# Feed-forward part in pairs of blocks, biases in pairs, all weights over one load queue, and a new instruction order, in an attention-plus-highway kernel

## The chip, the cores and the metric

The kernel runs on one core of a Trainium2 chip. A core has a matrix engine (TensorE, PE in the profile, with its weight loads as PEld), a vector engine (VectorE, DVE), a scalar engine (ScalarE, ACT), a general engine (GpSimd, POOL), a fifth engine that here only issues transfers (SyncE, SP), and 16 DMA engines that move data between the main memory (HBM), and the on-chip memory (SBUF). Matrix products land in PSUM, eight banks of 512 float32 columns on 128 partitions. The engines run at the same time, each in its own program order, and wait for one another on semaphores. The metric is the device time of one execution, in microseconds (us).

## The reference

```
q, k, v: [8 batches, 8 heads, 576 positions, 64]
scores = q k^T / 8 - slope[h] * |i - j|,   kept only where 0 <= i - j < 128
attn   = softmax(scores) v
x      = attn, heads side by side: [4608 tokens, 512]
H      = relu(x w_h)
T      = sigmoid(x w_t + b_t)
out    = T * H + (1 - T) * x                [4608, 512] float32
```

## The kernel before

**Tiling.** Two batches are done at a time (`m` = 0 to 3). Their 576 positions are five blocks of 128, 128, 128, 128 and 64 positions, and a block of queries meets only its own block of keys and the one before. The work of one `m` is cut into stages: `A` and `B` (key blocks 0-1 and 2-4), or, for `m` = 0, the smaller stages `a`, `b`, `c`, `d`. Within a stage the eight heads are taken two at a time (`g` = 0 to 3).

**Attention.** q and k are loaded by GpSimd's DMA queue, which turns float32 into bfloat16 on the way (`load_qk`, `load_tails` for the last 64 positions, `load_v`). `transposes` (`tr`) brings q and k to head-dimension-first by matrix transposes, `evac` (`te`) copies them out of PSUM on DVE or ACT. `scores` (`s`, L329) multiplies, both batches at once in two halves of 64 array rows each. `soft` (`exp`, L345, ACT) takes the exponential, `mask` (`msk`, L364, DVE) multiplies the band mask in, `pv` (L393) multiplies with v, which carries a column of ones for the sum, and `norm` (`nrm`, L409 and L410, DVE) divides and writes the attention output of one stage, the tile `x`.

**Feed-forward part.** When all heads of a stage are normalised, its blocks of 128 tokens go through, one block (`gi`) at a time:

- `f_x` (`xp`, L433, PE): four transposes of `x`; `f_xe` (`x`, L442, ACT): the copy out of PSUM;
- `f_h` (`h`, L449, PE): four matmuls with `w_h`; `f_u` (`u`, L456, DVE): relu, minus `x`;
- `f_z` (`z`, PE): four matmuls with `w_t` (L465) and a fifth (L467) that adds the bias `b_t` by multiplying a row of ones (`ones1`) with the bias row `bT`; `f_th` (`th`, L473, ACT): tanh;
- `f_t` (`t`, L478, GpSimd): tanh to sigmoid; `f_g` (`g`, L483, DVE): product with `u`; `f_out` (`o`, L489, GpSimd): plus `x`, to float32; `f_st` (`st`, L497 and L505, SP): four stores of 32 partitions each, or two for a last block of 64 positions.

For the second-last blocks of the last stage `t` is on DVE, and the very last `o` too.

**Weights.** `w_t` and `b_t` come over GpSimd's queue. `w_h` is loaded by SP as float32 into the buffer that will later hold the q of `m` = 1 (`wf`, L222), and ACT casts it to bfloat16 (`wc`, L228).

**Order.** Every step above is a node of a list. The program's order, on all engines together, is the written list `ISSUE` of node numbers, and the PSUM bank of each allocation is taken in turn from the written list `BANKS`. Both were made by a search with the planner's costs given in `node(...)`; on the chip only the order and the banks matter. So an engine never overtakes: a node that waits holds up all later nodes of its engine. The functions that the change touches:

Of the kernel before, what the change touches and what calls it, by code (L numbers as in the profile page):

```python
# [14 lines left out]
def kernel(  # L15
# [41 lines left out]
        "A": ((0,), (1,), (2,), (3,)), "B": ((0,), (1,), (2,), (3,), (4,)),  # L57
        "a": ((0,), (1,)), "b": ((0,), (1,)), "c": ((0,), (1,)), "d": ((0,), (1,), (2,)),
    }

# [77 lines left out]
    ones1 = cp.tile([P, P], BF16, name="ones1")  # L138
    wH = cp.tile([P, NCK, DM], BF16, name="wH")
# [51 lines left out]
    def c_vec():  # L191
        nc.vector.memset(ones1[:], 0.0)
        nc.vector.memset(ones1[0:1, :], 1.0)
        nc.vector.memset(bT[:], 0.0)
        for h in range(H):
            nc.vector.memset(cvec[:, h : h + 1], float(np.exp(-float(P) * slopes[h])))
# [20 lines left out]

    def w_stage():
        return QL[1][:].rearrange("p r h n -> p (r h n)").bitcast(F32)

    def load_wf():
        nc.sync.dma_start(  # L222
            out=w_stage().rearrange("p (c n) -> p c n", c=NCK),
            in_=moe_w_h.rearrange("(c p) n -> p c n", p=P),
        )

    def cast_wf():
        nc.scalar.copy(out=wH[:].rearrange("p c n -> p (c n)"), in_=w_stage())  # L228

    def load_w(n):  # L230
        if n == 2:
            nc.gpsimd.dma_start(out=bT[0:1, :], in_=moe_b_t.rearrange("(o n) -> o n", o=1))
        else:
            nc.gpsimd.dma_start(
                out=(wH, wT)[n][:],
                in_=(moe_w_h, moe_w_t)[n].rearrange("(c p) n -> p c n", p=P),
            )
# [177 lines left out]

    def grp(m, kind, gi):
        bs = GROUPS[kind][gi]
# [9 lines left out]
    def f_x(m, kind, gi):  # L427
# [3 lines left out]
        for i in range(n):  # L431
            for c in range(NCK):
                nc.tensor.transpose(  # L433
                    out=pt[:, c * P : (c + 1) * P], in_=x[:, i, c * P : (c + 1) * P],
# [3 lines left out]
    def f_xe(m, kind, gi):  # L438
# [4 lines left out]
            out=xt[:, 0:n].rearrange("p i c n -> p i (c n)"), in_=TR[m, kind, gi][:, 0:512].rearrange("p (i n) -> p i n", i=1)  # L443
        )

    def f_h(m, kind, gi, i):
        AH[m, kind, gi] = ps_tile(1)
        for c in range(NCK):
            nc.tensor.matmul(out=AH[m, kind, gi], lhsT=XT[m, kind, gi][:, i, c, :],  # L449
                             rhs=wH[:, c, :], start=c == 0, stop=c == NCK - 1)  # L450

    def f_u(m, kind, gi):
# [4 lines left out]
            out=uu[:, 0:n, :], in0=AH[m, kind, gi].rearrange("p (i n) -> p i n", i=1), scalar=0.0, in1=x,  # L457
            op0=ALU.max, op1=ALU.subtract,
        )

    def f_z(m, kind, gi, i):
        AZ[m, kind, gi] = ps_tile(1)
        az = AZ[m, kind, gi]
        for c in range(NCK):
            nc.tensor.matmul(out=az, lhsT=XT[m, kind, gi][:, i, c, :], rhs=wT[:, c, :],  # L465
                             start=c == 0, stop=False)
        nc.tensor.matmul(out=az, lhsT=ones1[:], rhs=bT[:], start=False, stop=True)  # L467

    def f_th(m, kind, gi):
# [3 lines left out]
        nc.scalar.activation(out=tt[:, 0:n, :], in_=AZ[m, kind, gi].rearrange("p (i n) -> p i n", i=1), func=ACTF.Tanh,  # L473
# [11 lines left out]
    def f_out(m, kind, gi, eng):  # L485
        bs, n, x = grp(m, kind, gi)
        ot = op.tile([P, 2, DM], F32, name="ot")
        OT[m, kind, gi] = ot
        eng.tensor_tensor(out=ot[:, 0:n, :], in0=UU.pop((m, kind, gi))[:, 0:n, :], in1=x, op=ALU.add)  # L489

    def f_st(m, kind, gi):
        ot, bs = OT.pop((m, kind, gi)), GROUPS[kind][gi]
# [17 lines left out]
    MODES = {"s": (1, 1), "tr": (2, 2), "pvB": (0, 2), "pvd": (0, 2)}  # L510
# [13 lines left out]
    node(("wf",), "SP", 450, -200, load_wf, land=2700)  # L524
    node(("wc",), "ACT", 2200, 2 * T, cast_wf, [("wf",)])
# [17 lines left out]
    def EV(m, w, part):  # L543
# [4 lines left out]
    HALF = {"A": (215, 1118, 1320, 370, 950), "B": (225, 1118, 1320, 800, 1080),  # L548
            "a": (130, 690, 790, 150, 640), "b": (130, 690, 790, 280, 640),
            "c": (130, 690, 790, 280, 640), "d": (160, 690, 790, 520, 800)}  # L550
# [7 lines left out]
    for m in range(ND):  # L558
# [4 lines left out]
        def qk(x=None, hs=None):  # L563
            for w in (0, 1):
# [4 lines left out]
                            lambda m=m, w=w: load_qk(m, w, x, hs), free + [("wc",)] * (m == 1 and w == 0)))  # L569
# [12 lines left out]
        if m == 0:  # L582
# [3 lines left out]
            for n_ in (1, 2):  # L586
                seq.append((("w", n_), 850, 2650 if n_ == 1 else 10, 1, lambda n_=n_: load_w(n_), []))
# [28 lines left out]
        for kind in ORDER[m]:  # L616
# [53 lines left out]
            for gi, bs in enumerate(GROUPS[kind]):  # L670
# [12 lines left out]
                for i in range(n):  # L683
                    node(("h", kb, i), "PE", 800, t + 0.4 * i * dt, lambda kb=kb, i=i: f_h(*kb, i),
                         [("x", kb), ("wc",), ("h", kb, 0)][: 2 + i], take=None if i else 1,
                         uses=[("x", kb)], keep=None if i else "uu")
                node(("u", kb), "DVE", (690, 1220)[two], t + 0.2 * dt, lambda kb=kb: f_u(*kb),
                     [("h", kb, n - 1)], take="uu", uses=[("h", kb, 0), xo])
                for i in range(n):
                    node(("z", kb, i), "PE", 1080, t + (0.5 + 0.4 * i) * dt,  # L690
                         lambda kb=kb, i=i: f_z(*kb, i),
                         [("h", kb, i), ("w", 1), ("w", 2)] + [("z", kb, 0)] * i,
                         take=None if i else 1, uses=[("x", kb)], keep=None if i else "tt")
                node(("th", kb), "ACT", (600, 1120)[two], t + 0.6 * dt, lambda kb=kb: f_th(*kb),
                     [("z", kb, n - 1)], take="tt", uses=[("z", kb, 0)])
                e, cost = ("DVE", (350, 500)) if last and gi else ("POOL", (750, 1350))
# [3 lines left out]
                node(("g", kb), "DVE", (500, 800)[two], t + 0.9 * dt, lambda kb=kb: f_g(*kb),  # L700
                     [("u", kb), ("t", kb)], uses=[("u", kb), ("th", kb)])
                end = last and gi == len(GROUPS[kind]) - 1
                e, cost = ("DVE", (640, 1150)) if end else ("POOL", (1250, 2350))
# [88 lines left out]
```

The softmax here doesn't subtract the row's maximum and nothing guards it: scores larger than these inputs give would overflow.

## Time and profile before

| | |
|---|---|
| median of 3 runs | 175.18 us (175.17 to 175.36) |
| the profiled execution's own time | 175.22 us |
| its span, first to last instruction | 173.5 us |
| PE busy | 150.3 us, 87% |
| DVE, ACT, POOL busy | 140.0, 125.4, 118.1 us |
| moved by GpSimd's queue, by SP's | 14.68 MB, 10.49 MB |
| granted TensorE clock | 0.987 |

Busy time is a sum over instructions. PE's includes the tail of each pipelined matmul, so a PE that is shown busy is not at its peak. The distance from one matmul's start to the next one's is the better measure of what it costs.

### The profile page before, as it was taken

To read this page: it belongs to the slowest core of one execution; us is meant where nothing else is said; L and a number is where in the kernel's file an instruction comes from. 1 tells how busy PE (TensorE), PEld (TensorE's weight loads), DVE (VectorE), ACT (ScalarE), POOL (GpSimd) and SP (SyncE) were. 2 spreads that over 40 slices of the span, in tenths; PEclk is the share of its full clock that TensorE was granted. 3 is DMA by queue.
4 is the path that set the end of the run, shared out by engine and by line. 5 is a ranking of instruction groups with operands and counts; after the bars stand their busy time and mean duration, and the time that the engine had idled before them with its cause. 6 is when DMAs were issued, how large, how long until landed. Compare 5 with 4: busy or idle time off the path is not lost.

```text
span 173.5 us, 5255 instructions
## 1 busy us (share of the span) xinstructions
PE 150.3 (87%) x2132; PEld 92.8 (54%) x2132; DVE 140.0 (81%) x244; ACT 125.4 (72%) x178; POOL 118.1 (68%) x132
## 2 busy tenths in 40 slices
PE   0169789999799789999999979999999999999930
PEld 0158544666566347766556755566556556754410
DVE  5087686999898888999867999889887899976580
ACT  2625678797799969899779968799898897235510
POOL 7997373488883799984067985884485969676540
PEclk9999999999999999999999999999999999999995
DMA  4999999999999999999999996793124332454443
GB/s 161 211 191 191 154 197 185 184 176 102 190 205 202 197 108 158 216 217 210 252 118 154 153 179 97 88 135 99 45 64 121 76 90 68 107 127 113 125 121 91
DMA packets 70167, 25.50 MB, mean 147 GB/s; under 512 B 48128, under 2 KB 65024, under 8 KB 70144
## 3 DMA queue, kind: packets, MB, share of 16 engines
q0 software_dynamic: 62832, 14.68, 120.7%
q1 hardware_dynamic: 7312, 10.49, 22.6%
q8 instruction: 16, 0.26, 0.7%
q14 instruction: 7, 0.06, 0.1%
HBM read 30.41 MB, written 9.44 MB: 230 GB/s over the span
## 4 chain that ended last, share of the span: by engine, by line
PE 53%; DMA 29%; DVE 5%; POOL 4%; ACT 3%; issue 2%; SPq 0%; POOLq 0%; ACTq 0%; DVEq 0%
DMA va<-in_v_dram 17%; PE ps L465 14%; PE ps L449 14%; DMA ktl<-in_k_dram 8%; PE ps L393 7%; PE ps L329 7%; PE ps L271 4%; PE ps L433 4%; DMA kl<-in_k_dram 3%; PE ps L467 3%; ACT pt L345 2%; DVE pt L364 1%; POOL kl L113 1%; DVE uu L456 1%; DMA out_dram<-ot 1%
## 5 line engine op out<-in xcount | busy, mean ns | idle before, releaser
L345 ACT ACTIVATE pt<-ps,bias 128x1024 bf16<-128x1024 f32 (+1 forms) x80 | 72.2, 950 | 13.5 <-PE ps L329 13.2
L489 POOL TENSOR_TENSOR ot<-uu,x 128x512 f32<-128x512 bf16 x35 | 47.7, 1365 | 24.9 <-DVE uu L483 24.8
L364 DVE TENSOR_TENSOR pt<-pt,mk 128x2048 bf16<-128x2048 bf16 (+1 forms) x40 | 46.5, 1174 | 0.8 <-ACT pt L345 0.8
L465 PE MATMUL ps<-wT,xt 128*128 128x512 bf16 x144 | 37.0, 379 | 1.0 <-DVE uu L456 0.8
L449 PE MATMUL ps<-wH,xt 128*128 128x512 bf16 x144 | 37.0, 386 | 0.3 <-DVE qt L290 0.3
L473 ACT ACTIVATE tt<-ps 128x512 f16<-128x512 f32 x36 | 21.6, 602 | 13.0 <-PE ps L467 11.9
L456 DVE SCALAR_TENSOR_TENSOR uu<-ps,x 128x512 bf16<-128x512 f32 x36 | 24.5, 684 | 4.6 <-PE ps L449 4.3
L329 PE MATMUL ps<-qt,kt 64*128 64x256 bf16 (+2 forms) x384 | 24.8, 248 | 3.4 <-DVE qt L290 1.1
L478 POOL TENSOR_SCALAR tt<-tt 128x512 f16<-128x512 f16 x32 | 21.8, 687 | 7.7 <-ACT tt L473 7.5
L410 DVE TENSOR_TENSOR x<-ps,rd 128x256 bf16<-128x256 f32 (+3 forms) x40 | 25.5, 638 | 1.4
L125 POOL DMA_DIRECT2D va<-in_v_dram x20 | 22.3, 1115 | 5.6 <-DMA ql<-in_q_dram 4.2
L393 PE MATMUL ps<-va,pt 128*128 128x65 bf16 (+1 forms) x576 | 24.9, 197 | 0.8 <-DMA va<-in_v_dram 0.7
L393 PEld LDWEIGHTS <-pt 128*128 128x128 bf16 (+1 forms) x576 | 21.1, 101 | 8.2 <-issue 2.9
L442 ACT COPY xt<-ps 128x512 bf16<-128x512 bf16 x36 | 20.7, 589 | 5.3 <-PE ps L433 5.1
L483 DVE TENSOR_TENSOR uu<-uu,tt 128x512 bf16<-128x512 bf16 x36 | 19.1, 538 | 4.3 <-POOL tt L478 4.1
L449 PEld LDWEIGHTS <-xt 128*128 128x128 bf16 x144 | 13.0, 99 | 14.3 <-issue 2.1
L465 PEld LDWEIGHTS <-xt 128*128 128x128 bf16 x144 | 12.9, 98 | 13.6 <-issue 1.5
L329 PEld LDWEIGHTS <-kt 64*128 64x128 bf16 x384 | 13.2, 96 | 12.9 <-issue 8.9
L271 PE MATMUL ps<-ident,kl 128*64 128x128 bf16 (+1 forms) x320 | 12.3, 228 | 8.1 <-DMA kl<-in_k_dram 7.9
L296 ACT COPY kt<-ps 128x1024 bf16<-128x1024 bf16 x13 | 13.0, 1020 | 5.4 <-PE ps L271 5.4
L271 PEld LDWEIGHTS <-kl 128*64 128x64 bf16 (+1 forms) x320 | 9.9, 126 | 10.1 <-DMA kl<-in_k_dram 8.4
L290 DVE COPY qt<-ps 128x1024 bf16<-128x1024 bf16 x16 | 11.0, 686 | 3.8 <-PE ps L271 3.7
(44 smaller groups left out, 125.5 us busy)
## 6 DMA issues: line engine op xcount, KB each, us to landing
out_dram<-ot SPq DMA_DIRECT2D x128, 64.0 KB, 2.4
va<-in_v_dram POOLq DMA_DIRECT2D x16, 256.0 KB, 14.2
ql<-in_q_dram POOLq DMA_DIRECT2D x3, 1024.0 KB, 16.0
kl<-in_k_dram POOLq DMA_DIRECT2D x3, 1024.0 KB, 15.7
ql<-in_moe_w_h_dram SPq DMA_DIRECT2D x1, 1024.0 KB, 5.2
out_dram<-ot SPq DMA_DIRECT2D x8, 128.0 KB, 2.4
kl<-in_k_dram POOLq DMA_DIRECT2D x4, 128.0 KB, 5.5
ql<-in_q_dram POOLq DMA_DIRECT2D x4, 128.0 KB, 5.9
```

Of the source, the lines that this page charges most:

```text
L125: nc.gpsimd.dma_start(out=VA[m % 2][0:n, c, :, :, 0:D].rearrange("s r h d -> s (r h) d"), in_=v[2 * m : 2 * m + 2, :, c * P : c * P + n, : ...
L271: nc.tensor.transpose(out=pt[r * D : (r + 1) * D, c : c + n], in_=L[ps, r, nh * hs + hl, t * D : (t + 1) * D], identity=ident[ps, ps],)
L329: nc.tensor.matmul(out=sc[:, r, o + off : o + off + w_], lhsT=KT[i][rows, h, j * P : (j + 1) * P], rhs=rhs, start=not add, stop=not add or ...
L345: nc.scalar.activation(out=PT[m, home, h // 2][:, h % 2, :, c0 : c0 + W], in_=SC[m, kind, h][:, :, o : o + W], func=ACTF.Exp, bias=BIAS[:, ...
L364: nc.vector.tensor_tensor(out=o, in0=o, in1=mk.to_broadcast([P, 2, rep, W]), op=ALU.mult,)
L393: nc.tensor.matmul(out=av[rows, hl, n * (D + 1) : (n + 1) * (D + 1)], lhsT=pt[:, hl, r, off : off + (D if narrow else P)], rhs=va[:, j, r, ...
L410: nc.vector.tensor_tensor(out=x.rearrange("p b (h d) -> p h b d", h=2), in0=av[:, :, :, 0:D], in1=rd[:, :, 0:nb].to_broadcast([P, 2, nb, D ...
L449: nc.tensor.matmul(out=AH[m, kind, gi], lhsT=XT[m, kind, gi][:, i, c, :], rhs=wH[:, c, :], start=c == 0, stop=c == NCK - 1)
L456: nc.vector.scalar_tensor_tensor(out=uu[:, 0:n, :], in0=AH[m, kind, gi].rearrange("p (i n) -> p i n", i=1), scalar=0.0, in1=x, op0=ALU.max ...
L465: nc.tensor.matmul(out=az, lhsT=XT[m, kind, gi][:, i, c, :], rhs=wT[:, c, :], start=c == 0, stop=False)
L478: eng.tensor_scalar(out=tt, in0=tt, scalar1=0.5, scalar2=0.5, op0=ALU.mult, op1=ALU.add)
L489: eng.tensor_tensor(out=ot[:, 0:n, :], in0=UU.pop((m, kind, gi))[:, 0:n, :], in1=x, op=ALU.add)
```

## The change

The blocks of a stage are taken two at a time through the feed-forward part (`GROUPS`), except in the last stage (`GROUPS_END`), where they stay single. A pair has one `x` copy of 1024 columns, one `u`, one `th`, one `t` and one `g` of double width; its `h` and its `z` each take two PSUM banks. The output sum `o` stays one instruction per block, and the store of a pair is four transfers of double size.

The bias of a pair is no longer a fifth matmul per block. A new step `zb` starts both banks with two matmuls of 64 array rows each, one in each half of the array; the bias row is loaded twice, to partitions 0 and 64 of `bT`, and `hot2` holds ones there. Single blocks keep the fifth matmul.

`w_h` is loaded by GpSimd's queue, cast on the way; the SP load `wf` and ACT's cast `wc` are gone, and with them the wait of the q load of `m` = 1 for the cast.

The last block of the last stage (3,B,4) does its `z`, `th`, `t`, `g`, `o` and store in two column halves of 256.

`ISSUE` and `BANKS` are new: 683 nodes instead of 762, 210 bank allocations instead of 252. The order differs from the first load on: GpSimd's loads begin with the second half of q of `m` = 0, `w_h` and the megabyte of k of `m` = 1 stand ahead of `w_t`, and v's block 1 stands behind `w_t`. The program ends with block (2,B,2), not (3,B,4).

```diff
     GROUPS = {
-        "A": ((0,), (1,), (2,), (3,)), "B": ((0,), (1,), (2,), (3,), (4,)),
-        "a": ((0,), (1,)), "b": ((0,), (1,)), "c": ((0,), (1,)), "d": ((0,), (1,), (2,)),
+        "A": ((0, 1), (2, 3)), "B": ((0, 1), (2, 3), (4,)),
+        "a": ((0, 1),), "b": ((0, 1),), "c": ((0, 1),), "d": ((0, 1), (2,)),
     }
+
+    GROUPS_END = ((0,), (1,), (2,), (3,), (4,))
...
+        nc.vector.memset(hot2[:], 0.0)
+        for i in range(2):
+            nc.vector.memset(hot2[i * D : i * D + 1, :], 1.0)
...
-    def load_wf():
-        nc.sync.dma_start(
...
-    def cast_wf():
-        nc.scalar.copy(out=wH[:].rearrange("p c n -> p (c n)"), in_=w_stage())
-
     def load_w(n):
         if n == 2:
-            nc.gpsimd.dma_start(out=bT[0:1, :], in_=moe_b_t.rearrange("(o n) -> o n", o=1))
+            for i in range(2):
+                nc.gpsimd.dma_start(
+                    out=bT[i * D : i * D + 1, :], in_=moe_b_t.rearrange("(o n) -> o n", o=1)
+                )
...
     def f_h(m, kind, gi, i):
-        AH[m, kind, gi] = ps_tile(1)
+        n = grp(m, kind, gi)[1]
+        if i == 0:
+            AH[m, kind, gi] = ps_tile(n).rearrange("p (i n) -> p i n", i=1) if n == 1 else ps_tile(n)
...
+    def f_zb(m, kind, gi):
+        AZ[m, kind, gi] = ps_tile(2)
+        for i in range(2):
+            rows = slice(i * D, (i + 1) * D)
+            nc.tensor.matmul(out=AZ[m, kind, gi][:, i, :], lhsT=hot2[rows, :], rhs=bT[rows, :],
+                             start=True, stop=False)
+
     def f_z(m, kind, gi, i):
-        AZ[m, kind, gi] = ps_tile(1)
-        az = AZ[m, kind, gi]
+        one = grp(m, kind, gi)[1] == 1
+        if one:
+            AZ[m, kind, gi] = ps_tile(1).rearrange("p (i n) -> p i n", i=1)
+        az = AZ[m, kind, gi][:, i, :]
         for c in range(NCK):
             nc.tensor.matmul(out=az, lhsT=XT[m, kind, gi][:, i, c, :], rhs=wT[:, c, :],
+                             start=one and c == 0, stop=not one and c == NCK - 1)
+        if one:
+            nc.tensor.matmul(out=az, lhsT=ones1[:], rhs=bT[:], start=False, stop=True)
...
+    def e_z(m, kind, gi, hf):
...
+        for c in range(NCK):
+            nc.tensor.matmul(out=az, lhsT=XT[m, kind, gi][:, 0, c, :], rhs=wT[:, c, half(hf)],
                              start=c == 0, stop=False)
-        nc.tensor.matmul(out=az, lhsT=ones1[:], rhs=bT[:], start=False, stop=True)
+        nc.tensor.matmul(out=az, lhsT=ones1[:], rhs=bT[:, half(hf)], start=False, stop=True)
...
-    def f_out(m, kind, gi, eng):
+    def f_out(m, kind, gi, i, eng):
         bs, n, x = grp(m, kind, gi)
-        ot = op.tile([P, 2, DM], F32, name="ot")
-        OT[m, kind, gi] = ot
-        eng.tensor_tensor(out=ot[:, 0:n, :], in0=UU.pop((m, kind, gi))[:, 0:n, :], in1=x, op=ALU.add)
+        if i == 0:
+            OT[m, kind, gi] = op.tile([P, 2, DM], F32, name="ot")
+        eng.tensor_tensor(out=OT[m, kind, gi][:, i, :], in0=UU[m, kind, gi][:, i, :],
+                          in1=x[:, i, :], op=ALU.add)
...
-    node(("wf",), "SP", 450, -200, load_wf, land=2700)
-    node(("wc",), "ACT", 2200, 2 * T, cast_wf, [("wf",)])
...
-                            lambda m=m, w=w: load_qk(m, w, x, hs), free + [("wc",)] * (m == 1 and w == 0)))
+                            lambda m=m, w=w: load_qk(m, w, x, hs), free))
...
-                e, cost = ("DVE", (350, 500)) if last and gi else ("POOL", (750, 1350))
+                e, cost = ("DVE", (350, 600)) if last and gi > 1 else ("POOL", (640, 1070))
...
-                end = last and gi == len(GROUPS[kind]) - 1
-                e, cost = ("DVE", (640, 1150)) if end else ("POOL", (1250, 2350))
+                end = last and gi > 2
+                e, cost = ("DVE", 640) if end else ("POOL", 1160)
```

The two written lists `ISSUE` and `BANKS` are replaced whole.

## The prediction

> **What bounds the kernel now.** I read the page's busy shares first, then its slices, then the chain, then the timeline of PE alone and of all engines in the last 25 us.
>
> ```profile
> PE 150.3 (87%) x2132; PEld 92.8 (54%) x2132; DVE 140.0 (81%) x244; ACT 125.4 (72%) x178; POOL 118.1 (68%) x132
> ...
> PE   0169789999799789999999979999999999999930
> ...
> DMA  4999999999999999999999996793124332454443
> ```
>
> PE is the fullest engine and idle for 23.2 us, of which the table by windows puts 8.2 in the first 10 us, 2.2 in 10 to 20, 0.9 in 20 to 30 and 7.3 after its last matmul at 166.2. Only about 4.5 us of idling lie between 40 and 160. So what counts is when PE starts, what it must do, where it stalls, and what follows its last matmul. The DMA row is full up to about 105 us (24 slices), so the loads are the second bound. The timeline of PE shows the two places where they still stop it after 40 us:
>
> ```profile
> 45.92 0.32 PE L393 MATMUL ps<-va,pt 128*64 128x65 bf16 x7 [0.73 <-DMA va<-in_v_dram]
> ...
> 57.83 0.39 PE L257 MATMUL ps<-ident,ktl 64*128 64x64 bf16 x8 [0.89 <-DMA ktl<-in_k_dram]
> ```
>
> The end, from the timeline of all engines: SP is still issuing the stores of earlier blocks when the last one needs it, and the last `o` is on DVE.
>
> ```profile
> 158.99 10.17 SPq L505 DMA_DIRECT2D out_dram<-ot  x20
> ...
> 168.05 0.69 DVE L489 TENSOR_TENSOR ot<-uu,x 128x512 f32<-128x512 bf16 x1
> 169.25 1.11 SPq L497 DMA_DIRECT2D out_dram<-ot  x2
> ```
>
> [...] Two 64-row scores matmuls of 256 columns run side by side, and the bias matmul of 512 columns takes 0.22 us to the next start when a 128-row operation follows, but 0.31 when the 64-row scores follow:
>
> ```profile
> 31.02 0.38 PE L467 MATMUL ps<-bT,ones 128*128 128x512 bf16 x1
> 31.33 0.61 PE L329 MATMUL ps<-qt,kt 64*128 64x256 bf16 x8
> ...
> 157.32 0.38 PE L467 MATMUL ps<-bT,ones 128*128 128x512 bf16 x1
> 157.54 0.39 PE L433 MATMUL ps<-ident,x 128*128 128x128 bf16 x4
> ```
>
> A switch thus costs 0.1 us. [...] SP's megabyte of `w_h` and the first k loads share the first 6 us. [...] Here ACT's 512-column tanh takes 602 ns and its 1024-column exponential 1119.
>
> **The change, part by part.** Orders are read from the written list against the list of nodes. The sum is made against the profiled execution: 175.22 us, of which 173.5 are span and 1.7 lie around it; its time is within 0.04 of the median.
>
> *Bias on PE: -3.0.* There are 14 pairs and 8 single blocks. Of 36 bias matmuls of 0.215 (start to start) 8 stay; 14 `zb` do two side by side, taken as 0.215 for both by the scores' example. 28 x 0.215 - 14 x 0.215 = 3.0. The last block's halves cost PE nothing: ten matmuls of 256 columns for five of 512.
>
> *Tile switches: +1.1.* Counting changes of shape along PE's order gives 130 before and 141 after: three `zb` have no scores beside them, eleven have them on one side, and other neighbours changed too. 11 x 0.1.
>
> *DVE, ACT, POOL: 0.* `u` falls from 36 x 684 ns to 14 of about 1220 (the DVE copy of 1024 columns) and 8 of 684, -2.0 us; ACT's tanh and copies lose about 3 and its cast 1.9; `t` and `g` become cheaper too. None of this is on the path: in the stretches where PE is full these engines have a fifth to a third of their time free. The cast ran at 6.08, when ACT had nothing else.
>
> *The start: +1.7.* All loads now run through GpSimd's queue, so `w_h` pushes back all behind it. By the landings in the trace a megabyte of q or k takes 5.0 to 5.6 us of that queue (25.8 to 31.4, 34.0 to 39.0), 256 KB of v 1.6 to 2.6, a weight 2.0 (23.8 to 25.8), a pair of tails 0.7 to 1.2. In the new order, with the first 512 KB in at about 8.5 (the first 128 KB landed at 6.7 while `w_h` was moving; that rivalry is gone), I get: first half of k complete at 15, of q at 17, v block 0 at 19, `w_h` 21.5, k of `m` = 1 at 28.4, `w_t` 30.7, v blocks 2 and 1 at 33 and 35.3, q of `m` = 1 at 40.6, v block 4 at 47. POOL issues a load only after the one eight before it has landed (the v load at 31.68 waited 4.18 us for q's landing at 31.4), and that does not delay these further. Following PE, ACT and DVE through the new order with the page's durations, PE begins at 8.5, as before; the first scores come at 14.2 instead of 13.0, since two q transposes and their copies on DVE stand first; then ACT's exponentials (0.61 each, 24 before the first pair's `th`) pace it, `pv(0,b,0)` waits some 1.4 us for v block 1, and the first q transposes of `m` = 1 about 1.1 for q. At 40.7 PE has by that order done 1.5 us less than before (missing: two `h`, one `z`; ahead: two scores, one transpose group), although it has saved 0.2 on one pair's bias: +1.7.
>
> *Stalls at 45.92, 47.5 and 57.8: -1.9* (0.73, 0.27, 0.89). The new order reaches `pv(0,d,0)` at about 48 to 50, with v in at 47, and puts the `m` = 2 tails later. What is late next is k of `m` = 2, at about 52.3, wanted at 53.
>
> *Stalls near the end: +1.15.* In the new order ACT does `th(3,A,1)`, a pair, ahead of the copy for (3,B,2). From the end of the last `z(3,A,1)` that is 1.12 + 0.6, and PE has only five transposes of 0.22 to fill it: 0.65 is left over. Further on `h(3,B,3)` uses bank 4 again, which `u(3,B,4)` must have read; DVE has `g(3,B,0)` ahead of that, which waits for POOL's `o(3,B,2)` of 1.15 and a `t`: about 0.5.
>
> *After the last matmul: +1.0.* The last block is now (2,B,2), with `t` and `o` on POOL. Counting from PE's end: tanh 0.6; on DVE `g(3,B,3)`, `u(2,B,2)`, `o(3,B,3)` come first, so its `g` ends at about 2.4 and POOL's `o` (1.15) at 3.6. SP has issued the four stores of (3,B,3) from 2.0 to 4.0 and then issues the last two, to 5.1; before it was done 4.15 after PE's end. The column halves of (3,B,4) save nothing, being no longer last.
>
> *PSUM: +1.0, chosen; -2.0 to +4.0.* Before shows no pair. A pair holds two banks for two `h` and a double `u` (about 3 us), and two more from `zb` to its tanh: about 13 bank-us where two single blocks took 7. Over 14 pairs that is some 90 of 8 x 150 bank-us. PE's remaining idling of 2.6 us between 60 and 160 could all but vanish, or each pair could add 0.3. I take a little over nothing, since no stall there is certain.
>
> Sum: -3.0 + 1.1 + 1.7 - 1.9 + 1.15 + 1.0 + 1.0 = +1.05, so 175.2 + 1.0 = **176.2 us**. The two loads that POOL now issues in addition (`w_h` 0.8, a second bias row 0.5) are in the start.
>
> **Rivals.** *Less PE work decides.* If PE stays as full as before and the order hides the loads, the bias is worth 3.0 - 1.1 = 1.9, the stalls at 46 to 58 another 1.9, and the start half its price (0.9) with the tail's 1.0: 175.2 - 1.9 - 1.9 + 0.9 + 1.0 = 173.3. For it: the idle table, in which little else than PE counts. Against: the loads, full for 24 slices and now half a megabyte longer on the one queue. It decides if PE idles less than about 3 us between 40 and its end. *PSUM or engine order becomes the bound:* 0.3 more per pair, 14 x 0.3 = 4 in place of 1: 179.2. For it: two-bank allocations beside the scores', which take two each as well. Against: ACT, DVE and POOL get lighter. *The bias pair doesn't run side by side:* then 14 x 0.215 comes back, 3.0 more, 179. Against: the scores do.
>
> **How the numbers follow.** A run of this kernel tells differences above 0.2% (0.35 us). Forecast case (loads and end eat the gain): 0.5; PE work decides: 0.33; PSUM or bias worse: 0.17. The forecast case's own range, 174.6 to 178, reaches into no change with a fifth of its chance. So faster 0.33, same 0.10, slower 0.57. The 8-in-10 range takes in the faster rival's middle and the upper bound of PSUM: 172.6 to 179.4.
>
> **What would show it.** In the profile after: nine bias matmuls of 128 rows (two of them halves) and 28 of 64 rows, these in twos within 0.22; PE busy 2 to 3 us lower; waits of PE for v and q loads between 32 and 42 us; PE's end near 166 and the span's end over 8 us after it, with POOL's `o` and SP's stores in between. A PE end below 164 refutes the start and the stalls; a PE idling by over 5 us between 60 and 160, with waits for `u` or `th`, says PSUM.

## The result, and the profile after

The changed kernel takes 175.09 us against 175.18 for the kernel before: a ratio of 0.9992 with an interval of 0.9971 to 1.0012. Run again beside other kernels, it gave 0.9998 (0.9968 to 1.0029). So by these comparisons the change makes no difference that can be told, where 176.2 had been forecast. Every comparison leaves out the executions more than 1.5% above the fastest of their kernel, and the changed kernel has more of these (7 of the 20 of its second series, 177.7 to 180.6 us, against 5 of the 31 of the kernel before beside it), so that by the medians of all executions there it is the slower one, 176.06 against 175.32.

The page of the changed kernel: the busy row of part 1, the slices of PE and of the DMA engines, and the instruction queue from part 3 (packets, MB, share of the 16 engines).

```profile
PE 149.0 (86%) x2137; PEld 92.2 (53%) x2137; DVE 132.8 (77%) x222; ACT 120.9 (70%) x150; POOL 117.3 (68%) x120
...
PE   0384869899699999899999999999999999999900
...
DMA  2999999999999999999499999997113134085453
...
q8 instruction: 16, 0.26, 0.6%
```

DVE, ACT and PE all did less, and the span is the same to 0.1 us (173.4 against 173.5). Where the time went is seen by adding PE's idling by stretch (stretch minus busy time):

| stretch | before | after | difference | the prediction's steps there |
|---|---|---|---|---|
| PE busy, whole span | 150.3 | 149.0 | -1.3 | -1.9 (bias -3.0, switches +1.1) |
| idle 0 to 40 us | 11.38 | 13.13 | +1.75 | +1.7 |
| idle 40 to 60 | 1.88 | 1.70 | -0.18 | -1.9 |
| idle 60 to 150 | 2.64 | 0.88 | -1.76 | +1.0 (PSUM) |
| idle 150 to 160 | 0 | 0.36 | +0.36 | +1.15 |
| after the last matmul | 7.3 | 8.34 | +1.04 | +1.0 |
| sum | | | -0.08 | +1.05 |

The windows from which the two large differences come, before and then after (stretch, its length, and the busy time of PE, PEld, DVE, ACT and POOL with their instructions; then granted clock, DMA share, GB/s):

```profile
40.00:60.00 20.00, 18.12 (x310) 11.86 (x309) 18.05 (x32) 17.38 (x24) 14.07 (x16) 1.00 2.20 181
60.00:100.00 40.00, 39.12 (x623) 24.93 (x622) 34.91 (x54) 34.66 (x43) 29.36 (x31) 1.00 2.51 176
100.00:150.00 50.00, 48.24 (x614) 29.25 (x610) 45.26 (x69) 41.36 (x56) 35.41 (x33) 1.00 0.59 98
```

```profile
40.00:60.00 20.00, 18.30 (x304) 11.41 (x301) 16.58 (x30) 17.38 (x20) 15.37 (x14) 1.00 2.11 171
60.00:100.00 40.00, 39.38 (x580) 24.08 (x578) 32.51 (x45) 33.47 (x37) 29.06 (x30) 1.00 1.72 166
100.00:150.00 50.00, 49.74 (x672) 29.99 (x671) 44.44 (x62) 38.68 (x39) 34.17 (x25) 1.00 1.16 104
```

Two lines of the table are wrong and nearly make up the miss: 40 to 60, where the gain did not come, and 60 to 150, where a loss was forecast and a gain came.

PE's waits in the changed kernel (total, times, longest):

```profile
PE ps L267 <- DMA ql<-in_q_dram: 8.0, 3, 7.1
PE ps L267 <- DMA kl<-in_k_dram: 2.3, 2, 2.0
PE ps L451 <- issue: 1.3, 1, 1.3
PE ps L389 <- DVE pt L360: 1.2, 2, 0.8
```

The first two and the last lie before 40 us. The third is the new one, a wait with no releaser ("issue": the engine waited for nothing that the profile shows). On PE's timeline it stands in the middle of four equal matmuls of one `h`:

```profile
43.37 0.82 PE L451 MATMUL ps<-wH,xt 128*128 128x512 bf16 x3
45.51 0.38 PE L451 MATMUL ps<-wH,xt 128*128 128x512 bf16 x1 [1.32 <-issue]
```

The first three had the same `xt`, `wH` and bank, so nothing that the kernel computes can be what the fourth waited for.

### The profile page after: what moved, and what is told of

Read it like the earlier page. It is cut to its first block, busy times and chain, and to the rows that moved or that the text cites. A ratio compares the mean times of both kernels' runs of the same rounds, so it can differ in the third digit from the quotient of the medians.

```text
span 173.4 us, 5098 instructions
## 1 busy us (share of the span) xinstructions
PE 149.0 (86%) x2137; PEld 92.2 (53%) x2137; DVE 132.8 (77%) x222; ACT 120.9 (70%) x150; POOL 117.3 (68%) x120
## 4 chain that ended last, share of the span: by engine, by line
PE 64%; DVE 10%; ACT 7%; DMA 6%; issue 5%; POOL 4%; SPq 1%; POOLq 1%; DVEq 0%; ACTq 0%
PE ps L451 17%; PE ps L477 15%; PE ps L325 9%; PE ps L389 8%; PE ps L267 8%; ACT pt L341 5%; DMA ql<-in_q_dram 5%; PE ps L432 3%; DVE x L406 3%; DVE pt L360 3%; POOL kl L115 2%; PE ps L468 2%; POOL ql L115 2%; DVE uu L458 1%; DMA out_dram<-ot 1%
## 5 line engine op out<-in xcount | busy, mean ns | idle before, releaser
L360 DVE TENSOR_TENSOR pt<-pt,mk 128x2048 bf16<-128x2048 bf16 (+1 forms) x40 | 42.7, 1087 | 4.1 <-ACT pt L341 4.0
L451 PE MATMUL ps<-wH,xt 128*128 128x512 bf16 x144 | 35.8, 380 | 1.5 <-issue 1.3
L477 PE MATMUL ps<-wT,xt 128*128 128x512 bf16 x140 | 35.3, 380 | 0.0
L531 POOL TENSOR_SCALAR tt<-tt 128x1024 f16<-128x1024 f16 (+1 forms) x19 | 20.4, 1074 | 18.8 <-ACT tt L526 17.0
L526 ACT ACTIVATE tt<-ps 128x1024 f16<-128x1024 f32 (+1 forms) x21 | 18.6, 885 | 15.8 <-PE ps L477 9.0
L458 DVE SCALAR_TENSOR_TENSOR uu<-ps,x 128x1024 bf16<-128x1024 f32 (+1 forms) x22 | 22.6, 1026 | 5.8 <-PE ps L451 4.3
L442 ACT COPY xt<-ps 128x1024 bf16<-128x1024 bf16 (+1 forms) x22 | 18.6, 857 | 3.2 <-PE ps L432 3.1
L267 PE MATMUL ps<-ident,ql 128*64 128x128 bf16 (+1 forms) x320 | 11.8, 228 | 8.0 <-DMA ql<-in_q_dram 8.0
L536 DVE TENSOR_TENSOR uu<-uu,tt 128x1024 bf16<-128x1024 bf16 (+1 forms) x21 | 13.6, 659 | 2.9 <-POOL tt L531 2.8
L267 PEld LDWEIGHTS <-ql 128*64 128x64 bf16 (+1 forms) x320 | 9.8, 126 | 8.9 <-DMA ql<-in_q_dram 8.2
L405 DVE RECIPROCAL rd<-ps 128x4 f32<-128x4 f32 (+3 forms) x40 | 7.9, 198 | 7.1 <-PE ps L389 6.5
```

Source lines behind the costliest of these rows:

```text
L267: nc.tensor.transpose(out=pt[r * D : (r + 1) * D, c : c + n], in_=L[ps, r, nh * hs + hl, t * D : (t + 1) * D], identity=ident[ps, ps],)
L360: nc.vector.tensor_tensor(out=o, in0=o, in1=mk.to_broadcast([P, 2, rep, W]), op=ALU.mult,)
L451: nc.tensor.matmul(out=AH[m, kind, gi][:, i, :], lhsT=XT[m, kind, gi][:, i, c, :], rhs=wH[:, c, :], start=c == 0, stop=c == NCK - 1)
L458: nc.vector.scalar_tensor_tensor(out=uu[:, 0:n, :], in0=AH[m, kind, gi], scalar=0.0, in1=x, op0=ALU.max, op1=ALU.subtract,)
L531: eng.tensor_scalar(out=tt, in0=tt, scalar1=0.5, scalar2=0.5, op0=ALU.mult, op1=ALU.add)
```

## The experiments

The theory after the result: each part does what it says, and the gain of the bias is eaten by the start, by the end and by the new stall. The rival: the parts are worth nothing, and one order was exchanged for an equal one. The expectations name what each run isolates by a word: PATH (the bias is on PE's path), ROUTE (the weights' queue), WIDTH (the double-width steps), START, TAIL, and FETCH (PE's own program arrives late). Ratios are to the kernel before, run beside each on the same chip. Where a diff shows `move`, the first step is put in the order just behind the second one.

### The bias of the pairs

```diff
-            nc.tensor.matmul(out=AZ[m, kind, gi][:, i, :], lhsT=hot2[rows, :], rhs=bT[rows, :],
-                             start=True, stop=False)
...
-        if one:
+        if True:
             nc.tensor.matmul(out=az, lhsT=ones1[:], rhs=bT[:], start=False, stop=True)
```

> The changed kernel with the bias of the 14 pairs added as before, by a fifth 128-row matmul per block (28 more of 0.215) in place of the 14 paired starts; banks and order stay. Theory PATH (PE sets the end nearly everywhere): 14 x 0.215 = 3.0 more, less the switches that the paired starts caused (0.1 to 0.2 each at the three without scores beside them, 0 to 0.1 at the others: 0.5 to 1): 177.1 to 177.6. Rival SLACK (PE's work is swallowed by its waits): under 1 us more.

Measured: 1.0266 (1.0215 to 1.0316). Its two best runs, 178.04 and 178.27, had a granted clock of 0.99; the other four, 180.4 to 180.9, had 0.98, so the ratio contains the clock as well. The span of the profiled execution (178.04) is 176.3, 2.9 longer than with `zb`: PE is busy for 2.2 us more and idle for 0.7 more, nearly all of it before 60 us. The busy time is what the path theory gives (2.0 to 2.5), and none of it is swallowed, so the pair bias is on the path. In the changed kernel's timeline of PE, a `zb` with scores behind it, and one with 128-row matmuls behind it:

```profile
83.56 0.39 PE L468 MATMUL ps<-bT,hot 64*128 64x512 bf16 x2
83.79 0.38 PE L325 MATMUL ps<-qt,kt 64*128 64x256 bf16 x4
...
123.64 0.39 PE L468 MATMUL ps<-bT,hot 64*128 64x512 bf16 x2
123.96 1.04 PE L477 MATMUL ps<-wT,xt 128*128 128x512 bf16 x4
```

0.23 us for both matmuls, 0.32 where 128-row matmuls come behind them. So the two run side by side (one 128-row bias matmul alone took 0.22), and the change of shape costs the 0.1 us that the prediction took.

### The route of `w_h`

In the changed kernel, `w_h` back on SP, cast by ACT, the rest of the order kept:

```diff
+        nc.sync.dma_start(
+            out=w_stage().rearrange("p (c n) -> p c n", c=NCK),
+            in_=moe_w_h.rearrange("(c p) n -> p c n", p=P),
+        )
+        nc.scalar.copy(out=wH[:].rearrange("p c n -> p (c n)"), in_=w_stage())
...
+    move(("w", 0), ("cbias",))
```

> The changed kernel with one part undone: w_h again comes over SP as float32 and is cast by ACT; everything else keeps its order. Theory ROUTE (the extra half megabyte on GpSimd's queue is what makes the start 1.75 us worse): the loads behind w_h land up to 2.0 us sooner, PE's idling before 40 us falls from 13.1 by 1 us or more, the time falls to 173.5 to 174.2. Rival ORDER (the new order of loads and of first steps costs it, not w_h's route): w_h's megabyte delays the first loads by 1 to 2 us, which gives back what it saves later, the time stays within 0.5 of 175.1.

In the kernel before, the reverse:

```diff
-    node(("wf",), "SP", 450, -200, load_wf, land=2700)
-    node(("wc",), "ACT", 2200, 2 * T, cast_wf, [("wf",)])
+    node(("wf",), "POOL", 450, -200, lambda: load_w(0), land=2700)
+    node(("wc",), "ACT", 2200, 2 * T, lambda: None, [("wf",)])
...
+    move(("wf",), ("w", 2))
```

> The kernel before with one part of the change alone: w_h over GpSimd's queue, cast on the way, issued right behind the bias row; SP's load and ACT's cast are gone. ROUTE: as in the prediction, all behind it lands 2 us later, time rises by 1 to 2 us (176.2 to 177.2). ORDER: the first loads land about 1.5 us sooner, the later ones about 0.5 later, the time stays within 0.5 of 175.2.

The second came as expected: 1.0092 (1.0066 to 1.0118), 1.6 us slower: in the profiled execution (178.51) PE begins earlier (4.62) and then waits for q's tails and v at 34.8, 36.3, 46.6 and 47.8 (0.81, 0.44, 0.32, 0.64). So GpSimd's queue is full enough for half a megabyte more to delay what is behind it. The first missed on both theories: 1.0146 (1.0098 to 1.0194), some 2.6 us slower. PE's timeline in the profiled execution (178.88):

```profile
8.86 1.76 PE L277 MATMUL ps<-ident,ql 64*64 64x64 bf16 x58 [8.86 <-DMA ql<-in_q_dram]
...
47.67 0.39 PE L461 MATMUL ps<-wH,xt 128*128 128x512 bf16 x1 [1.98 <-issue]
```

With the megabyte on SP, PE starts at 8.86 instead of 7.12, 1.74 us later, and what it waits for is the first q. The later loads landed no earlier (v block 1 at 35.8 instead of 35.7), and the stall without releaser was 0.7 longer. Of the 3.4 us by which this span is longer, 1.5 are idling in the first 10 us, 0.8 further idling up to 60 us, and 1.3 PE's busy time, which grew behind that stall (the granted clock from 40 to 60 us is 0.91; more on this below). Neither route is free, and each order is built around its own.

### The start

q's second half comes first in the new order, 512 KB. Here quarters of k and q come first, then second halves (`k0(1, ...)` is a load of k, `k0(0, ...)` of q), and the first transposes and scores follow that, five of them in other banks:

```diff
+    early = [("kpad", 0), ("vpad", 0), k0(1, 0, 1), k0(0, 0, 1), ("ident",), ("ones", 0), ("kpad", 1), k0(1, 0, 0),
+             k0(0, 0, 0), ("cbias",), ("trim",), ("cvec",), ("vpad", 1), k0(1, 1, None), ("tri",), ("mask0",), k0(0, 1, None)]
...
+    order = early + [k_ for k_ in order if k_ not in early]
...
```

> The changed kernel with the first loads and first steps in another order: the quarter loads of k and q (four) first, then the second half of k and of q; transposes, copies and the scores of stage a follow that order. Theory START (the 1.75 us of extra idling before 40 us come from the first 512 KB of q, which are needed last): first scores at about 9 to 10 instead of 12.5, and the time falls by 1 to 1.75. Rival LATER LOADS (v block 1 at 35.3 and q of m = 1 at 40.1 hold PE up whatever came before): PE waits longer there, the time falls by less than 0.4.

Measured: 1.0277 (1.0207 to 1.0348), 179.2 to 180.6. PE did begin at 4.63, and lost it again:

```profile
16.05 1.06 PE L267 MATMUL ps<-ident,kl 64*64 64x64 bf16 x32 [1.74 <-DMA kl<-in_k_dram]
...
19.28 1.92 PE L267 MATMUL ps<-ident,ql 64*64 64x64 bf16 x64 [2.16 <-DMA ql<-in_q_dram]
```

Idling from 10 to 20 us is 4.33 instead of 3.06, and before 40 us 14.9 instead of 13.1; the last of q and k of `m` = 0 landed at 19.24 instead of 17.11. The rest of the loss comes later: a stall of 2.07 at 49.10, and behind it 2.1 us more of PE's busy time. So the theory that the large first transfer costs the start is not borne out. That the start depends on when all of `m` = 0 is in, and not on the first matmul, fits these landings, but no run isolates it.

### The width of the pairs' steps

The pairs keep their banks, their order and their bias; only the `x` copy, `u`, `th` and `g` are issued as two instructions of 512 columns; of these only `th` is shown.

```diff
-        nc.scalar.activation(out=tt[:, 0:n, :], in_=AZ[m, kind, gi], func=ACTF.Tanh, scale=0.5)
+        for i in range(n):
+            nc.scalar.activation(out=tt[:, i, :], in_=AZ[m, kind, gi][:, i, :], func=ACTF.Tanh, scale=0.5)
...
```

> The changed kernel with the wide steps of its pairs cut in two again (the x copy and th on ACT, u and g on DVE: 56 more instructions, some 4 us more of DVE and 4 of ACT); t, o, stores, PE's work, order and banks stay. Theory WIDTH (between 60 and 160 us PE waits less than before because the pairs' wide steps leave DVE and ACT more slack): PE's idling there rises from 1.2 to 2.6 or more, time 176.5 or more. Rival ORDER (the new order is simply better filled there, and PE's cover hides the rest): within 0.5 of the changed kernel.

Measured: 1.0272 (1.0195 to 1.035), 179.5 and 180.0. But the largest stall in its profiled execution (182.56) was one without releaser, so the size of the width's part was open:

```profile
73.61 0.40 PE L325 MATMUL ps<-qt,kt 64*128 64x256 bf16 x2 [2.50 <-issue]
```

It was repeated with 64 idle transposes ahead of PE's first step (their purpose is told below):

> The changed kernel with the pairs' x copy, u, th and g each split into two instructions of single width, and with 64 idle transposes ahead of PE's first step, so that the fetches fall at other instructions than in the split run before. WIDTH: PE idles some 2 us more than with whole pairs between 60 and 150, in waits for qt, pt and uu, and the time is 175.5 to 177, that is 1.5 to 3 above the changed kernel with the same 64 transposes (174.1). FETCH ONLY (the split run's loss was its fetch stall): 174.0 to 175.0, with PE's idling between 60 and 150 under 1.2.

Measured: 1.0116 (1.0078 to 1.0154), 177.3 to 177.9; above the range given. The same kernel with whole pairs and the same transposes has 0.994, so the split costs some 3 us, or 2.3 by the medians of all runs (177.66 against 175.35); both were profiled at a granted clock of 0.94. PE's idling from 60 to 160 us is 3.38 against 1.56, and these waits are new or longer:

```profile
PE ps L389 <- DVE pt L360: 2.3, 5, 0.8
PE ps L325 <- DVE qt L286: 1.5, 3, 0.7
...
PE ps L325 <- DVE uu L458: 0.3, 1, 0.3
PE ps L389 <- DVE x L406: 0.3, 1, 0.3
```

All are for DVE. Its busy time rose from 133.3 to 141.4. So the wide steps are on the path in this order: a `u` of 1024 columns takes 1220 ns and two of 512 take 1372, one tanh 1027 and two 1202, so one double step was 152 and 175 ns shorter than two single ones. One reservation: the order was searched with wide steps in it, and another might carry narrow ones better.

Does DVE's load also explain the waits of the kernel before? There `g` was cut to half of the columns (256 of 512), with no pair and no new order; the other half of the output then lacks its factor:

```diff
-        nc.vector.tensor_tensor(out=uu, in0=uu, in1=TT.pop((m, kind, gi))[:, 0:n, :], op=ALU.mult)
+        tt = TT.pop((m, kind, gi))
+        nc.vector.tensor_tensor(out=uu[:, :, 0:256], in0=uu[:, :, 0:256], in1=tt[:, 0:n, 0:256], op=ALU.mult)
```

> The kernel before with the product g on the first half of each block's columns only (256 of 512; the other half of the output then lacks its factor): 36 DVE instructions of 538 ns become about 290, 9 us less DVE work than before, a little more than the 7.2 that the change took away. No pairs, no new order. LIGHT (DVE's load makes before's waits after 60 us): PE's idling between 60 and 160 falls from 2.6 to about 1.2, with the waits for uu at 63.3 and qt at 101.6 under 0.4 each, and the time is 173.6 to 174.5. ORDER (only the new order removed them): they stay, 174.9 to 175.4.

Measured: 0.9934 (0.9893 to 0.9974). `g` fell only to 396 ns, so DVE lost 4.3 us of its 140.0, not 9. The two waits in PE's timeline, in the kernel before and then in this one:

```profile
63.28 1.02 PE L465 MATMUL ps<-wT,xt 128*128 128x512 bf16 x4 [0.80 <-DVE uu L456]
...
101.59 0.40 PE L329 MATMUL ps<-qt,kt 64*128 64x256 bf16 x8 [1.13 <-DVE qt L290]
```

```profile
62.13 1.02 PE L465 MATMUL ps<-wT,xt 128*128 128x512 bf16 x4 [0.49 <-DVE uu L456]
...
100.07 0.40 PE L329 MATMUL ps<-qt,kt 64*128 64x256 bf16 x8 [1.12 <-DVE qt L290]
```

The first shrank from 0.80, the second stayed at 1.12. Idling from 60 to 160 fell by 0.37 only. The rest of the gain lies before 40 us (0.6), where the runs do not say why, behind the last matmul (0.4) and in PE's busy time (0.5). The largest single wait of before is thus a matter of where its q copies stand in DVE's order, not of how full DVE is. Both theories hold for one wait each; the drop of 1.76 in the changed kernel is not split any further by these runs.

### The stall without a releaser

The trace records the transfers of the instruction queue: 16 of 16 KB in each of the two kernels. PE has 2137 matmuls and as many weight loads in the changed kernel, 4274 or 267 for each transfer, while no other engine shows more than 222 instructions on the page; that the transfers are PE's program is thus an estimate so far. Eleven of the sixteen took 0.88 to 1.02 us. The one that began at 42.19 took 1.56, while a block of v was loading (it landed at 45.02) and the DMA row stood at 9; it ended at 43.75, and the stall 1.76 later. In the kernels with single biases and with the edits at the end, the stall stands ahead of the same matmul (1.28 at 45.87, 1.61 at 45.95). To move the fetches to other instructions without touching the work, 64 idle transposes (128 instructions, about half a fetch by that estimate) were put ahead of PE's first step, where PE waits for loads:

```diff
+    def filler():
+        for _ in range(64):
+            nc.tensor.transpose(out=PSB[0:P, 7, :].bitcast(BF16)[:, 0:P], in_=ident[:], identity=ident[:])
...
+    order.insert(order.index(("tr", 0, 0, (1, 0))), "fill")
```

> The changed kernel with 64 transposes of the identity into an unused bank ahead of PE's first step, while PE waits for the first load anyway: 128 more instructions on PE, no more work later. Theory FETCH (the stall of 1.3 us near 45, put down to no engine, is PE waiting for its own program: in the before, the changed and three other traces such a stall ends 1.3 to 1.8 us after a 16 KB transfer on the instruction queue[...]): the transfers come half a block earlier in PE's program and the stall near 45 goes or moves; the time changes by up to 1 us either way. Rival (a wait for DVE's copies or masks): the stall stays at the same scores step and the time within 0.3.

Measured: 0.994 (0.9899 to 0.9982), the profiled execution 173.87. The stall at 45.51 is gone, and there are 17 fetches, one more than the 16 of the changed kernel, so the queue does carry PE's program. A stall of 2.47 came at 14.72, where the changed kernel had waited 1.99 for k; from 40 to 60 PE idles 0.87 instead of 1.70. The granted clock in this trace is 0.5 from 13.6 to 30.6 us, but the steps there are no slower for it: the same 32 transposes of k take 1.92 us in both kernels there (at 28.35 and 28.49).

That might still be due to PE's having been active earlier. So two more kernels, with small transposes (64x64): 64 of them (128 instructions, taken again as half a fetch), and 128 (256 instructions, taken as a whole one), after which every fetch would meet the instruction that it met in the changed kernel.

> The same with 64 small idle transposes: 128 rows, half a fetch, as in the run with 64 large ones, but with a fifth of their work or less. FETCH: no stall over 0.6 labelled issue between 43 and 50; one of up to 2.5 near 14.7, where loads are waited for anyway; 173.8 to 174.5. WARM: less activity ahead, so less gain, 174.5 to 175.2, with the stall near 45 back.

> The changed kernel with 128 small idle transposes (64x64) ahead of PE's first step: 256 rows, exactly one 16 KB fetch, so that every later fetch ends at the same instruction as in the changed kernel, one fetch later in number. FETCH: the stall of 0.7 to 2.0 us labelled issue between 44 and 50 us is back, at the same step as in the changed kernel, and the time is that kernel's, 174.8 to 175.6. WARM (it is PE's earlier activity itself that gained the time, not the place of the fetches): the stall stays away and the time is 173.8 to 174.3, as with 64 idle transposes.

PE's timeline near 45 us, first with half a fetch, then with a whole one:

```profile
43.34 0.75 PE L267 MATMUL ps<-ident,ql 128*64 128x128 bf16 x20 [1.01 <-issue]
```

```profile
45.08 0.82 PE L451 MATMUL ps<-wH,xt 128*128 128x512 bf16 x3
47.72 0.38 PE L451 MATMUL ps<-wH,xt 128*128 128x512 bf16 x1 [1.82 <-issue]
```

With a whole fetch the stall is back in the same `h`, again ahead of its fourth matmul: 1.82 us, at a later time because everything was later. With half a fetch it stands earlier in the order, inside the q transposes, and is 1.01. That place decides between FETCH and WARM: it is the fetch.

A count in the traces shows the same without these two runs. Put PE's records of one trace (its matmuls, its weight loads and a few of its sequencer) in order of time and number them. In the changed kernel the stall near 45 us comes behind record 1217, and one of 0.46 at 71.10 behind record 1985, 3 x 256 later. Twelve of the sixteen traces have such stalls without a releaser of over 0.35 us, 22 in all, and each comes behind record 449, 705, 1217, 1473, 1985 or 2241, give or take two: always a multiple of 256 apart, whatever step of the kernel stands there. By these distances a fetch of 16 KB is 256 records. Taking 449 as the first of these places, PE passes the nth in no trace sooner than 1.33 us after the end of the nth transfer.

Behind a long stall more was lost than its length. PE's timeline in the second profile of the changed kernel (an execution of 179.35 us):

```profile
47.40 0.38 PE L451 MATMUL ps<-wH,xt 128*128 128x512 bf16 x1 [2.00 <-issue]
...
48.03 1.71 PE L451 MATMUL ps<-wH,xt 128*128 128x512 bf16 x4
```

The four matmuls of the next `h` take 1.71 us, where the first profile has 1.04 (at 46.14): the granted clock is 0.5 for 3.4 us from 48.3 on. The same 3.4 us at 0.5 stand in the profiles with `w_h` back on SP (from 49.1, stall 1.98), with the other first loads (from 50.0, stall 2.07 at the same record) and with the split steps (from 73.2, stall 2.50). After the stalls of 1.28 to 1.82 at that place (changed kernel, single biases, edits at the end, whole fetch) the clock stayed at 1. That the long stall brings the clock down is likely from this, but no run isolates it.

The rest of what was expected of the two runs with small transposes missed. 128 transposes ran until about 9.9 us, held up the start and met a fetch there too (0.72 at 12.93 and 1.54 at 19.67), so the kernel took 1.0179 (1.0132 to 1.0226), not the 1.0 of FETCH. And half a fetch did not take the stall near 43 below 0.6, although it gave 0.9916 (0.9882 to 0.995). The median of all its 20 runs is 175.4, and of all 12 with the large transposes 175.35, so the place of the stall is shown, and the gain in time is not firm.

Does the same lie behind the 0.73 at 45.92 in the kernel before, put down to v? A fetch there began at 42.42 and took 2.24.

> The kernel before with the same 64 idle transposes ahead of PE's first step: 128 rows of PE's program, half of a 16 KB fetch. In before the fetch that began at 42.42 took 2.24 us, and PE stood 0.73 us at 45.92, put down to v's load. FETCH: the fetches move to other instructions; the stall at 45.92 goes or falls under 0.3, PE's idling between 40 and 60 falls from 1.9 to about 1.1, and 174.2 to 174.9 result, unless a new fetch stall falls into a full stretch. LOAD: the stall is v's load, stays at 0.5 to 1.0, and the time stays within 0.3% of before.

Measured: 1.0017 (0.9996 to 1.0038), no change. The stall at 45.92 is gone, yet this does not speak for FETCH: v's landing stayed (45.9 before, 45.7 here), and PE came to that `pv` later, at 46.7, after two stalls without releaser at 16.25 (0.80) and 23.55 (1.20). The 0.73 was v's load, as the profile says. It also covered the slow fetch: held by v until 45.92, PE of the kernel before came to the fourth of the counted places only at 46.35, 1.70 us after that fetch had ended (44.65).

### The end

In the changed kernel, `t` and `o` of (2,B,2) on DVE, and the stores of (3,B,3) issued by ACT:

```diff
+        eng = nc.scalar if (m, kind, gi) == (3, "B", 3) else nc.sync
...
-                     lambda kb=kb, v=e == "DVE": f_t(*kb, nc.vector if v else nc.gpsimd),
+                     lambda kb=kb, v=e == "DVE" or kb == (2, "B", 2): f_t(*kb, nc.vector if v else nc.gpsimd),
...
-                         lambda kb=kb, i=i, v=end: f_out(*kb, i, nc.vector if v else nc.gpsimd),
+                         lambda kb=kb, i=i, v=end or kb == (2, "B", 2): f_out(*kb, i, nc.vector if v else nc.gpsimd),
...
```

> The changed kernel with two edits at its end: t and o of the last block (2,B,2) on DVE instead of GpSimd, and the four stores of (3,B,3) issued by ACT instead of SP. The prediction's step for the end (o on GpSimd and SP's queue, both about 1 us late): the end after PE's last matmul falls from 8.3 to about 7.2 us, time 174.0. Rival (the end is set by the landing of the stores, which are the same bytes): no change.

Measured: 0.9959 (0.9928 to 0.999), and in the profiled execution (176.04) 7.86 us instead of 8.34 after the last matmul; the median of all 14 runs is 175.26, so the gain shows at the end of the profile and not in every comparison of times. The end of the changed kernel in the timeline of all engines (SPq is SP's queue of issues):

```profile
165.29 3.83 SPq L559 DMA_DIRECT2D out_dram<-ot  x8
...
165.78 0.83 POOL L531 TENSOR_SCALAR tt<-tt 128x512 f16<-128x512 f16 x1 [0.86 <-ACT tt L526]
...
167.75 1.15 POOL L542 TENSOR_TENSOR ot<-uu,x 128x512 f32<-128x512 bf16 x1 [1.14 <-DVE uu L536]
169.22 1.11 SPq L551 DMA_DIRECT2D out_dram<-ot  x2
```

The last stores are issued at 169.22, when SP has just finished eight others (169.12) and POOL has finished `o` (168.9): two chains of one length, so both had to be taken away. With both gone, the end is DVE's, which now has `t`, `u`, `g` and two `o` in a row: its last `o` starts at 169.07, and the last stores are issued from 169.79 on. The gain is 0.5, not the whole 1.0.

At last both edits with the 64 large transposes:

> The changed kernel with 64 idle 128-column transposes ahead of PE's first step, and with the two edits at the end (t and o of (2,B,2) on DVE, the stores of (3,B,3) issued by ACT). If the instruction fetch (FETCH) and the end (TAIL) are separate costs, the gains add: about 1.0 us for the first (174.1 against 175.1) and 0.5 for the second, so 173.3 to 173.9, a ratio of 0.989 to 0.993 to the kernel before; the stall near 45 us absent, and 7.9 instead of 8.3 us after PE's last matmul. If the gain of the first is only in where the noise of the loads fell (CHANCE), 174.5 to 175.2.

Measured: 0.9878 (0.983 to 0.9926), from three of the six runs. The six go from 172.05 to 175.99 with a median of 174.9, so it is the best version found, 1.2% below the kernel before by the comparison and 0.2% by the median of all. In the profiled execution (175.89) there is a stall of 1.06 at 44.77, at the q transposes where half a fetch had put it.

And the changed kernel, unaltered, in the same company:

> The changed kernel as it is, as the yardstick for the runs beside it: 175.1, and as in its first profile PE's last matmul ends at about 165.1, 8.3 us before the end of the span, with a stall of about 1.3 us near 45 us that the profile puts down to no engine.

Its ratio was given at the head. The stall ahead of the fourth matmul of that `h` is there again, the 2.00 at 47.40 shown above.

## Why the prediction was wrong

- **Bias on PE and tile switches, right in size.** Together they had been put at -1.9. Taking `zb` out costs 2.2 us of PE's busy time and 2.9 of span; a pair takes 0.23 us, a switch 0.1. From the kernel before to the changed one PE's busy time fell by 1.3 only, and the runs do not say where the other 0.6 is.
- **The start, right.** +1.75 against +1.7, and the landings came as worked out: v block 1 at 35.7 (35.3 had been given), q of `m` = 1 at 40.4 (40.6), v block 4 at 46.8 (47). The first 512 KB were in at 7.1, not 8.5, and PE began at 7.12; the second wait for k (1.99) took that back. Which part of the new order costs it stays open: `w_h` back on SP and the other first loads both made the start worse.
- **Stalls at 45.92, 47.5 and 57.8: -1.9. This step failed, by 1.7.** The three went as forecast. "What is late next" had been sought among the loads of data, where k of `m` = 2 was indeed on time (it landed at 51.7, and PE's transposes of it began at 54.34 without a wait). It was PE's own program, 1.32 at 45.51. That a fetch can be slow while the loads run (1.56 us at 42.19, with the DMA row at 9) was not in the sum.
- **PSUM: +1.0. This step failed, by 2.8.** The measured value is -1.76, close to the lower bound of -2.0. Behind it stands another step, *DVE, ACT, POOL: 0*, with its reason that they had a fifth to a third of their time free (from 60 to 150 us it was 11% on DVE, 16% on ACT and 28% on POOL). An average share does not say that no wait ends on them: in before 0.80 for `uu` and 1.13 for `qt` did, both named in the waits by engine. Of these the first follows DVE's load and the second its order (the lightened kernel before). And in the changed kernel the wide steps are worth 2 to 3 us (split against whole, both with the idle transposes), about as much as the bias; 1.8 of that is idling between 60 and 160 us.
- **Stalls near the end: +1.15. The first was there, the second not.** The stall behind `th(3,A,1)` is 0.27 and, after four transposes, 0.26 more until `h(3,B,2)`: 0.53 for the 0.65 worked out, of which the idle table sees 0.36. Bank 4 was free in time for `h(3,B,3)`, since PE went on without a gap from 152.93.

PE and ACT at that place in the changed kernel:

```profile
151.12 1.06 PE L432 MATMUL ps<-ident,x 128*128 128x128 bf16 x16
152.45 0.38 PE L432 MATMUL ps<-ident,x 128*128 128x128 bf16 x4 [0.27 <-ACT tt L526]
152.93 1.90 PE L451 MATMUL ps<-wH,xt 128*128 128x512 bf16 x8
```

```profile
151.37 1.02 ACT L526 ACTIVATE tt<-ps 128x1024 f16<-128x1024 f32 x1 [5.15 <-PE ps L477]
152.29 2.19 ACT L442 COPY xt<-ps 128x512 bf16<-128x512 bf16 x4
```

- **After the last matmul, right:** +1.04 against +1.0, by POOL's `o` and SP's stores together, as described; the run with both edits at the end shows that 0.5 of it is to be had that simply.

So the sum of the forecast had its gains and losses in the right places but for two, and these partly cancelled: 1.7 of gain did not come, 3.5 of loss did not either (2.76 and 0.79), and with PE's 0.6 the forecast was 1.1 too high. That the total lies so near is luck. Of the rivals, *less PE work decides* had set its condition as PE idling less than 3 us between 40 and its end: it idled 2.94, and yet 173.3 did not come, because the start cost its full price and the fetch took 1.3. The rivals of PSUM pressure and of bias matmuls one behind the other are refuted.

## What to carry to other kernels

Price the waits that end on an engine, not its share of busy time: DVE, with 19% of its time free before, held up PE here by 0.80 and 1.13 us, the second where its order put the needed step late. When a stall without a releaser stands between equal matmuls, look in the trace for the instruction queue, count the engine's instructions between such stalls, and see whether the stall moves when idle instructions are put where the engine waits anyway; do so before crediting an order with it or blaming it. And of an end with two chains of one length, shorten both, then look for the third.

## What the runs showed of the hardware

The instruction queue carries PE's program: 128 more instructions made a 17th fetch of 16 KB (16 in the changed kernel) and moved the place of the stall. In the changed kernel eleven fetches took 0.88 to 1.02 us and the others up to 1.60; the slowest named here took 2.24 (kernel before, at 42.42) and 2.50 (split kernel, at 69.46). The 2.24 and the 1.56 at 42.19 came with the DMA row at 9, but in the kernel before 1.46 (at 117.11) came with the row at 3, so a full row is not the whole cause. PE stood 0.5 to 2.5 us (in one place although its fetch took no longer than usual: 12.22 + 0.89, stall of 2.47 to 14.72, with the large idle transposes), its stall ending some 1.3 to 1.8 after the fetch of that moment (42.19 + 1.56, stall to 45.51; in the split kernel 69.46 + 2.50, stall to 73.61). These places lie multiples of 256 of PE's records apart in every trace that has them; the fetch of 2.24 us at 42.42 in the kernel before stopped nothing, as PE came to its place 1.70 after its end. With the four stalls of 1.98 to 2.50 us past 40 us the granted clock went to 0.5 for 3.4 us. Why PE goes on only 1.3 us or more after the recorded transfer, and whether the stall itself brings the clock down, these runs do not show.
